# Splitting the four-chunk cache loads of a decode kernel between the queues of SyncE and ScalarE

## The chip, the cores and the metric

The kernel runs on one core of one Trainium2 chip. The metric is the time of one execution on the device, in microseconds (us). Before the change it was 2488.25 us, the median of 3 runs (2488.16 to 2488.78). The engines are written as in the profile: PE (TensorE matmul), PEld (its weight load), DVE (VectorE), ACT (ScalarE), POOL (GpSimd) and SP (SyncE). SPq and ACTq are the instruction queues of SP and ACT where they issue transfers; the transfers themselves run on 16 DMA engines that the core has.

## What is computed

Two rounds of the same two layers on a decode step with batch B = 2, width D = 512: an attention layer over a long cache (32 query heads, 8 heads of K and V, 32768 keys, head width 128), then a small mixer.

```python
x = x + A(layernorm(x))      # A: grouped-query attention over the cache
x = x + M(layernorm(x))      # M: LayerNorm, one token mixed to F = 1792 hidden, gelu, back
x = x + A(layernorm(x))
x = x + M(layernorm(x))

def A(x):
    q = (x @ wq)                                  # 32 heads of 128
    scores = einsum("bhqd,bhkd->bhqk", q, k) * 128 ** -0.5
    o = einsum("bhqk,bhkd->bhqd", softmax(scores), v)
    return o @ wo
```

All values are float32. K and V of one batch and one cache head are 16.8 MB each, and there are 16 such pairs, 537 MB; both rounds read the whole cache (small parts are kept on the chip between the rounds), so that 1061 MB come in over the DMA engines.

## The kernel before

**Units and chunks.** The work on one pair of batch and cache head in one layer is a unit `n`, 0 to 31. Its K and its V are cut into 8 chunks of 4096 keys, 2.1 MB each (`CK`, 16 KB in each of 128 partitions). PE multiplies each K chunk with the unit's queries (`k_chunk`, L481, into `scores`), and each V chunk with the exponentials of the scores (`v_chunk`, L638, into `acc`). On the page, one matmul of the program is two instructions, so a chunk is 16 of them.

**Loads.** All chunks lie in one large tile, `mem`. `load_k` and `load_v` pick cells of it and call `load` (L188), which issues one transfer on SP. In the first part of the program (K of units 0 to 12, V of 0 to 11) and in the last (K of 21 to 31, V of 20 to 30 and the first of 31) a load brings four chunks, 64 KB to a partition; two cell groups (cells 0 to 3, cells 4 to 7) take turns. In the middle part the loads are of one to three chunks and go to more cells. The last V is loaded as four chunks, two chunks, and then five pieces of a half chunk and less (`PIECES`). Weights of two heads at a time are loaded on SP as well (L129, and 32 KB pieces of them at L142).

**Order.** The order of the program is written out by hand. `stream` is the list of loads, sorted by a key; the last loop of the kernel takes one load after the other, issues it, then emits its chunks on PE, and after each chunk `run(t)` emits the other steps that are due at that time: `at(time, step, ...)`. Every engine executes its own instructions in this order. An issue of a transfer therefore stands, on the engine that issues it, behind all that this engine was given before; it also waits by semaphores until PE has read out what lies in the cells.

**One round in the first and last part.** There K of a unit and V of the unit before it alternate. I count positions in chunks from the begin of a unit's K; a round is 16 positions long, for K of unit n+1 and V of unit n:

| position | load issued there | PE reads | ACT is given, after that chunk |
|---|---|---|---|
| 0 to 4 | Ka: K chunks 0 to 3 | them | at 4: exps(n,1), exponentials of the second half of the scores of n |
| 4 to 8 | Va: V chunks 0 to 3 | them | |
| 8 to 12 | Kb: K chunks 4 to 7 | them | |
| 12 to 16 | Vb: V chunks 4 to 7 | them | at 14: exps(n+1,0), those of the first half of n+1 |

A step "at 4" is emitted after the chunk that ends at 4 and ahead of the load that is issued at 4. `exps` is `exponentials` (L518): four activations and four reads of their accumulator on ACT. exps(n+1,0) needs the maximum of all scores of n+1, which two small products on PE give, `max_1` (at 13) and `max_2` (at 14, L510); exps(n,1) needs the transposed scores (`turn_scores`, L516, DVE, at 4), whose tile is free once Vb has been read. Ka and Kb lie in one cell group, Va and Vb in the other. At 0 to 3 there is also the output of the unit before (`out_0` to `out_2`), from 10 on the queries of the next unit (`make_q`). After the last unit of a pair of layer and batch the mixer's gelu tiles (`hidden_tile`, L889, one a position) come on ACT too.

**The end.** The last unit is 31. exps(31,1) are given to ACT when V of unit 30 has been read (`t1 = ahead`), before the load of V chunks 0 to 3 of unit 31 is emitted. After the last V piece come the last output and the last mixer (`last_out`, `last_mixer`).

Of the kernel before, what the change touches and what calls it, by code (L numbers as in the profile page):

```python
# [14 lines left out]
CK = 4096  # L15
# [3 lines left out]
PACK = 4  # L19
# [30 lines left out]
def gqa_mixer_kernel(ctx: ExitStack, tc: tile.TileContext, x, kt, v, wqo, cols, out):  # L50
# [17 lines left out]
    nc = tc.nc  # L68
# [104 lines left out]
    loaded, seen = [0], {0: 0}  # L173
# [12 lines left out]
        return loaded[0] - seen[-(-t // 1)] + (-t) % 1 if t <= now[0] else 0  # L186

    def load(t, src):  # L188
        nc.sync.dma_start(t, src)
        loaded[0] += t.shape[-1] / CK  # L190

    def buffer(m, limit, until):

# [256 lines left out]
    def load_k(n, c, m, limit):  # L450
        layer, b, h = unit_of(n)
        stay = h == keeper and c in KEPT_K
        until = k_done[n, c + m - 1]
        if stay:
            for j in range(m):
                hold(KEPT_K[c + j], 1, k_done[units.index((1, b, h)), c + j])
            bufs = [cells(KEPT_K[c], m)]
        elif limit == RING:
            bufs = spread(m, until, n in (N1 + 1, N2 + 1) and m == 1)
        else:  # L460
            bufs = [buffer(m, limit, until)]
        src, f = piece(kt, b * HKV + h, c, m), 0
        for t in bufs:
            if not (stay and layer):
                load(t, src[:, f : f + t.shape[-1]])
            f += t.shape[-1]
        at = [q for t in bufs for q in quads(t)]
        for j in range(m):
            k_at[n, c + j] = at[j * (JT // QT) : (j + 1) * (JT // QT)]
# [81 lines left out]
    def load_v(n, c, m, limit):  # L551
# [7 lines left out]
        if stay and m > 1:  # L559
            k = KEPT[c][1]  # L560
            own = cells(k, m)
            load(own, src)
            for j in range(m):
                hold(k + j, 1, v_done[units.index((1, b, h)), c + j])
                v_at[n, c + j] = quads(cells(k + j))
            return
        if stay:
            if layer == 0:
                load(own, src[:, :f])
                for j in range(2 if stay > QT else 1):  # L570
                    busy[2 * KEPT[c][1] + j] = v_done[units.index((1, b, h)), c]
            if stay == JT // QT:
                v_at[n, c] = at
                return
            bufs = [half(until)[:, : CK - f]]
        elif limit == RING:
            bufs = spread(m, until, False, PLACE_V.get((n - N1, c)))
        else:
            bufs = [buffer(m, limit, until)]
# [405 lines left out]
    kbeg, k_done, vbeg, v_done, vend_of, v_from, v_to, brings, starts, t = {}, {}, {}, {}, {}, {}, {}, [], [], 0  # L985
# [171 lines left out]
    t = 0  # L1157
# [83 lines left out]
```

## Time and profile before

| what | value |
|---|---|
| median of 3 runs | 2488.25 us |
| span of the profiled execution, first to last instruction | 2486.6 us |
| PE busy | 1413.2 us (57%) |
| DVE busy | 256.6 us (10%) |
| ACT busy | 185.5 us (7%) |
| read from HBM | 1061.19 MB, 427 GB/s over the span |
| chain that ended last, DMA's share | 72% |

The profile is one execution, taken by the hardware profiler; its own time lies 1.65 us under the median of the runs. The page shows the span in 40 slices with the DMA engines' busy share and rate, the queues, the chain of work that ended last, and the costliest groups of instructions. Other views of the same trace list the transfers of a stretch (DMA), the instructions in order of time (timeline), the chain piece by piece, and busy time by stretch (windows). A timeline row reads: start, duration, engine, line, operation, result <- operands, count, and in brackets the idle time before it with what ended it. A row with SPq is the issue of a transfer, not its duration. Sizes in the DMA view are left out for the largest transfers.

### The profile page before, as it was taken

How to read it: one execution, taken by the hardware profiler on the slowest of the kernel's cores; microseconds unless marked ns; L12 is line 12 of the kernel's file. 1: busy time of each engine (PE TensorE's matmuls, PEld its weight loads, DVE VectorE, ACT ScalarE, POOL GpSimd, SP SyncE). 2: the span in 40 equal slices, each digit the busy share in tenths (PEclk: the TensorE clock that was granted, in tenths of full speed). 3: DMA queues.
4: the chain of work that ended last, by engine and by line, in shares of the span. 5: the costliest groups of instructions: out<-in, count | busy, mean ns of one | idle time of the engine just before them, and what ended most of it. 6: DMA issues, size and time to landing. Idle time of an engine off the chain costs nothing.

```text
span 2486.6 us, 20856 instructions
## 1 busy us (share of the span) xinstructions
PE 1413.2 (57%) x9438; PEld 386.1 (16%) x9438; DVE 256.6 (10%) x659; ACT 185.5 (7%) x544; POOL 4.9 (0%) x17
## 2 busy tenths in 40 slices
PE   4544545556555454657677675455555664456546
PEld 1111111111111111112122121111111111111112
DVE  1000000000000000003113110000000000010002
ACT  0000000000000000002012000000000000011002
POOL 0000000000000000000000000000000000000000
PEclk8777777776777777888888887777677777777878
DMA  9999999999999999999999999999999999999996
GB/s 421 434 433 429 433 437 430 434 436 431 427 435 431 436 427 432 431 429 412 431 433 415 429 432 432 434 435 430 436 429 429 429 435 434 428 436 431 434 435 287
DMA packets 30594, 1062.54 MB, mean 427 GB/s; under 512 B 3749, under 2 KB 3753, under 8 KB 4394
## 3 DMA queue, kind: packets, MB, share of 16 engines
q1 hardware_dynamic: 30216, 1061.17, 99.2%
q8 instruction: 74, 1.21, 0.2%
q14 instruction: 14, 0.11, 0.0%
q10 hardware_dynamic: 290, 0.04, 0.0%
HBM read 1061.19 MB, written 0.00 MB: 427 GB/s over the span
## 4 chain that ended last, share of the span: by engine, by line
DMA 72%; PE 26%; DVE 0%; issue 0%; another core or an unknown queue 0%; ACT 0%; SPq 0%; ACTq 0%
DMA mem<-in_v_dram 61%; PE acc L638 20%; DMA mem<-in_kt_dram 10%; PE scores L481 3%; DMA mem<-in_wqo_dram 2%; PE kept L162 1%; PE kept L395 1%; PE small L669 0%; PE small L510 0%; PE bcast L395 0%; PE small L797 0%; PE small L504 0%; PE kept L296 0%; PE kept L849 0%
## 5 line engine op out<-in xcount | busy, mean ns | idle before, releaser
L481 PE MATMUL scores<-mem,small_sb 128*32 128x512 f32 x4096 | 615.7, 724 | 544.5 <-DMA mem<-in_kt_dram 544.4
L638 PE MATMUL acc<-mem,S 128*16 128x512 f32 x4088 | 621.3, 737 | 473.0 <-DMA mem<-in_v_dram 471.3
L481 PEld LDWEIGHTS scores<-mem,small_sb 128*32 128x32 f32 x4096 | 147.2, 127 | 914.6 <-issue 839.2
L521 ACT ACTIVATE S<-S,small_sb 128x128 f32<-128x128 f32 x232 | 119.3, 518 | 1974.6 <-DVE small_sb L512 1377.0
L638 PEld LDWEIGHTS acc<-mem,S 128*16 128x16 f32 x4088 | 132.6, 110 | 839.6 <-issue 699.1
L496 DVE TENSOR_REDUCE small_sb<-scores 128x1 f32<-128x512 f32 x64 | 44.3, 692 | 743.8 <-PE scores L481 743.8
L516 DVE STREAM_TRANSPOSE S<-scores 128x512 f32<-128x512 f32 x64 | 45.5, 710 | 141.4 <-PE acc L638 137.2
L395 PE MATMUL kept<-mem,small_sb 128*2 128x512 f32 x96 | 54.5, 691 | 3.9 <-DMA mem<-in_wqo_dram 2.1
L296 PE MATMUL kept<-mem,small_sb 128*1 128x512 f32 (+1 forms) x236 | 42.1, 597 | 2.7 <-ACT mem L892 2.4
L521 ACT ACTIVATION_READ_ACCUMULATOR S<-S,small_sb 128x1 f32 x232 | 43.3, 187 | 0.0
L506 DVE TENSOR_REDUCE small_sb<-small 1x4 f32<-1x128 f32 x32 | 8.9, 279 | 294.1 <-PE small L504 294.1
L671 DVE RECIPROCAL small_sb<-small 128x4 f32<-128x4 f32 x32 | 5.9, 185 | 321.6 <-PE small L669 321.6
L680 DVE TENSOR_TENSOR small_sb<-small,small_sb 128x4 f32<-128x4 f32 x31 | 5.1, 164 | 299.1 <-PE small L678 299.1
L608 DVE SCALAR_TENSOR_TENSOR S<-acc,small_sb,S 128x128 f32<-128x128 f32 x93 | 32.6, 351 | 3.3
L892 ACT ACTIVATE S<-bcast,small_sb 128x512 f32<-128x512 f32 x28 | 21.6, 778 | 89.9 <-DVE small_sb L761 87.8
L606 DVE TENSOR_SCALAR S<-acc,small_sb 128x128 f32<-128x128 f32 x31 | 10.8, 350 | 146.7 <-PE acc L638 146.7
L162 PE MATMUL kept<-mem,small_sb 48*2 48x512 f32 x32 | 25.2, 929 | 0.0
L421 PE MATMUL small<-small_sb,mem 2*128 2x2 f32 x112 | 14.7, 248 | 17.9 <-DVE mem L417 17.9
L395 PE MATMUL bcast<-mem,small_sb 128*1 128x512 f32 (+1 forms) x40 | 20.9, 640 | 0.0
L678 PEld LDWEIGHTS small<-small_sb,S 128*128 128x128 f32 x62 | 13.2, 266 | 48.7 <-issue 41.9
L797 PE MATMUL small<-small_sb 128*128 128x128 f32 x120 | 18.7, 290 | 0.0
L504 PE MATMUL small<-small_sb 128*1 128x128 f32 x64 | 16.7, 354 | 3.3 <-DVE small_sb L502 3.3
(154 smaller groups left out, 340.9 us busy)
## 6 DMA issues: line engine op xcount, KB each, us to landing
mem<-in_kt_dram SPq DMA_DIRECT2D x14, 4096.0 KB
mem<-in_v_dram SPq DMA_DIRECT2D x11, 4096.0 KB
mem<-in_v_dram SPq DMA_DIRECT2D x13, 2048.0 KB
mem<-in_kt_dram SPq DMA_DIRECT2D x12, 2048.0 KB
mem<-in_kt_dram SPq DMA_DIRECT2D x24, 1024.0 KB
mem<-in_v_dram SPq DMA_DIRECT2D x21, 1024.0 KB
mem<-in_wqo_dram SPq DMA_DIRECT2D x4, 3840.0 KB
mem<-in_wqo_dram SPq DMA_DIRECT2D x3, 4096.0 KB
```

What stands on the lines that cost most here:

```text
L162: nc.tensor.matmul(q_ps[n][:B, :], low[:, j * B : (j + 1) * B], lowered[h][:, j * D : (j + 1) * D], start=(j == 0), stop=False,)
L296: nc.tensor.matmul((rows if to is None else to)[32 * g : 32 * g + b + 1, :], weights if b else weights[:, 1:], row, start=to is not None, ...
L395: nc.tensor.matmul(q_ps[n][:m, :], xnT[:, d, b : b + m], wq_at(h, d), start=(d == 0 and h not in lowered), stop=(d == last),)
L481: nc.tensor.matmul(sc_ps[n, half][32 * g : 32 * g + 32, :], q, kc[k * NG + g], start=(i == 0 and k == 0), stop=(i == PACK - 1 and k == SUB ...
L496: nc.vector.tensor_reduce(mx[n][:, half : half + 1], sc_ps[n, half], axis=AX.X, op=ALU.max)
L504: nc.tensor.matmul(pm[:1, :P], mxa, ident, start=True, stop=True)
L516: nc.vector.transpose(S[half], sc_ps[n, half])
L521: nc.scalar.activation(s[:, :, h], s[:, :, h], AF.Exp, bias=neg[n][:, h : h + 1], scale=SCALE, accum_out=lsum[n][:, half, h : h + 1],)
L608: nc.vector.scalar_tensor_tensor(t, acc[:, k * DH : (k + 1) * DH], mask[:, k : k + 1], t, op0=ALU.mult, op1=ALU.add)
L638: nc.tensor.matmul(acc[32 * g : 32 * g + R * QT, :], S[half][:, col : col + R * QT], vc[q], start=(c == v_from[n] and q < NG), stop=(c == ...
L797: nc.tensor.matmul(p[:, :P], ident, ident, start=True, stop=True)
L892: nc.scalar.activation(hid[key, f], px[key], AF.Gelu_apprx_tanh, bias=shift[key][:, f : f + 1], scale=slope[key][:, f : f + 1],)
```

## The change

`load` splits a load of four chunks into two halves by columns: the first two chunks are issued on SP as before, the other two on ACT. The destination cells, the source and all other loads are the same.

```diff
     def load(t, src):
-        nc.sync.dma_start(t, src)
-        loaded[0] += t.shape[-1] / CK
+        w = t.shape[-1]
+        if w == PACK * CK:
+            nc.sync.dma_start(t[:, : w // 2], src[:, : w // 2])
+            nc.scalar.dma_start(t[:, w // 2 :], src[:, w // 2 :])
+        else:
+            nc.sync.dma_start(t, src)
+        loaded[0] += w / CK
```

So each half has a transfer and a completion of its own: rows of 32 KB, 128 of them, 4.2 MB. The issue on ACT stands in ACT's order at the position of the load in the table above. In the texts below Ka1 is the half of Ka on SP and Ka2 the half on ACT, and so on; V01, V23, V45 and V67 are the chunk pairs of the last V.

## The prediction

> **What bounds the kernel now.** I read the page first (span, DMA row, queues), then the DMA view in three stretches, then the timeline of two loads in the middle, then the chain at the end.
>
> ```profile
> span 2486.6 us, 20856 instructions
> ...
> PE 1413.2 (57%) x9438; PEld 386.1 (16%) x9438; DVE 256.6 (10%) x659; ACT 185.5 (7%) x544; POOL 4.9 (0%) x17
> ...
> DMA  9999999999999999999999999999999999999996
> GB/s 421 434 433 429 433 437 430 434 436 431 427 435 431 436 427 432 431 429 412 431 433 415 429 432 432 434 435 430 436 429 429 429 435 434 428 436 431 434 435 287
> ...
> q1 hardware_dynamic: 30216, 1061.17, 99.2%
> ...
> L892 ACT ACTIVATE S<-bcast,small_sb 128x512 f32<-128x512 f32 x28 | 21.6, 778 | 89.9 <-DVE small_sb L761 87.8
> ```
> ```profile
> mem<-in_kt_dram SPq DMA_DIRECT2D x48
> mem<-in_v_dram SPq DMA_DIRECT2D x47
> ```
>
> The DMA row is 9 in every slice but the last, one queue carries 99.2%, and the rate stays near 432 GB/s. The kernel is bound by bytes. The two rows without a size are the loads that the change splits: 48 of K and 47 of V, 128 rows of 64 KB each, 8.39 MB a load, 797 MB of the 1061. The stretch 100 to 1000 us has, apart from weights, nothing but them; the stretch 1440 to 1530 us has nothing but 4 MB loads, in 32 KB rows, which is the very shape of a half; 1140 to 1200 us is mostly 1 MB loads in 8 KB rows:
>
> ```profile
> DMA packets 7033, 389.13 MB, mean 432 GB/s; under 512 B 824, under 2 KB 824, under 8 KB 824
> ```
> ```profile
> DMA packets 1408, 38.77 MB, mean 431 GB/s; under 512 B 160, under 2 KB 160, under 8 KB 160
> ...
> mem<-in_kt_dram SPq DMA_DIRECT2D x6, 4096.0 KB
> mem<-in_v_dram SPq DMA_DIRECT2D x3, 4096.0 KB
> ```
> ```profile
> DMA packets 3242, 24.67 MB, mean 411 GB/s; under 512 B 359, under 2 KB 359, under 8 KB 359
> ...
> mem<-in_v_dram SPq DMA_DIRECT2D x10, 1024.0 KB
> ```
>
> So 432 GB/s with 64 KB rows, 431 with 32 KB rows, 411 only where rows are far shorter. Half a load alone is 4.194 MB / 432 GB/s = 9.7 us, two halves that share the engines 19.4 us.
>
> Why do the engines never run dry? One unit in the middle (Vb, then Ka, Va, Kb of the next; positions as in the section on the kernel):
>
> ```profile
> 1806.14 0.38 PE L510 MATMUL small<-small_sb 1*128 1x4 f32 x2
> 1806.45 3.63 PE L638 MATMUL acc<-mem,S 128*16 128x512 f32 x32
> ...
> 1808.80 0.19 ACT L521 ACTIVATION_READ_ACCUMULATOR S<-S,small_sb 128x1 f32 x1
> 1810.14 0.33 SPq L189 DMA_DIRECT2D mem<-in_v_dram  x1
> ...
> 1819.89 3.64 PE L481 MATMUL scores<-mem,small_sb 128*32 128x512 f32 x16 [9.81 <-DMA mem<-in_kt_dram]
> ...
> 1827.13 3.61 PE L481 MATMUL scores<-mem,small_sb 128*32 128x512 f32 x32
> ...
> 1830.80 0.33 SPq L189 DMA_DIRECT2D mem<-in_kt_dram  x1
> ...
> 1832.24 0.52 ACT L521 ACTIVATE S<-S,small_sb 128x128 f32<-128x128 f32 x1 [23.25 <-DVE S L516]
> ...
> 1834.16 0.19 ACT L521 ACTIVATION_READ_ACCUMULATOR S<-S,small_sb 128x1 f32 x1
> ...
> 1839.57 3.18 PE L638 MATMUL acc<-mem,S 128*16 128x512 f32 x16 [8.84 <-DMA mem<-in_v_dram]
> ...
> 1849.23 0.33 SPq L189 DMA_DIRECT2D mem<-in_v_dram  x1
> ...
> 1859.23 5.32 PE L481 MATMUL scores<-mem,small_sb 128*32 128x512 f32 x32 [10.06 <-DMA mem<-in_kt_dram]
> ...
> 1870.62 0.33 SPq L189 DMA_DIRECT2D mem<-in_kt_dram  x1
> ...
> 1887.41 0.19 ACT L521 ACTIVATION_READ_ACCUMULATOR S<-S,small_sb 128x1 f32 x1
> ```
>
> Each SPq row is a load issued the moment PE has read its buffer out: 1810.14, 1830.80, 1849.23. The load ahead of it lands some 9 us later (PE starts on it at 1819.89, 1839.57, 1859.23). So the queue holds about 9 us of work whenever a new load joins it. SP can do that because it has nothing else to wait for.
>
> **The change part by part.** *What is removed and added.* 95 issues of SP become 95 of SP and 95 of ACT, 0.33 us each by the SPq rows; ACT is busy 7%, and 95 x 0.33 = 31 us spread over the span lies in its idle time. No byte is added. The rows of these loads go from 64 to 32 KB, which the stretches above price at 432 against 431 GB/s: 797 MB take 1845 or 1849 us. I take **+3 us**, and keep 0 to 7 us (7 for what rounding and the stretch's edges hide).
>
> *Two queues at once* are not in this trace. The slices that hold nothing but these loads run from 427 to 437 GB/s: at 437 the 797 MB would take 1824 us, 21 us less, at 427 1866 us, 21 us more. I take neither: the one queue keeps the 16 engines busy for 99.2% of the span, so there is no pause for a second to fill, and the bytes are the same. As to how the engines share, I take turns row by row, since the profile counts a packet for each row: 1408 packets less the 160 tiny ones are 1248 for 38.77 MB, 31 KB each. So two queues that both have work get half the rate each.
>
> [...]
>
> *The order in which ACT issues* is the real edit. SP still runs ahead, and earlier than now, since half a buffer is free after two chunks. ACT issues in program order behind its exponentials. At position 14 stands exps(n,0), before the issue of the next Ka's second half (Ka2); at 4 stands exps(n,1), before the issue of Va2 and of Kb2, behind it. By the rows, exps(n,0) ends 2.8 us after the products of position 14 (1806.14 to 1808.99), and exps(n,1) 3.6 us after Ka is read (1830.74 to 1834.35). A Ka is now issued at 1870.62; its half on ACT would have to wait for exps that end at 1887.60, 17 us later. A Va is now issued at 1810.14; its half would wait until 1834.35, 24 us later. In the other direction nothing is held up: when ACT comes to Ka2, Va2 or Kb2 the buffer has been read, and behind Vb2, which does wait for PE (position 8), only the exps of position 14 are queued. Where the 14 gelu tiles of a mixer (778 ns each) are spread over the positions after 3, each waits for PE at an earlier position than the issue behind it, so I add nothing. On SP nothing is moved past anything; the weight loads find a shorter queue.
>
> Do the engines run dry? Prices: a half from a cold PE 5.3 us (1859.23, 32 instructions), a hot one 3.6 (1827.13), Kb's second half 6.1 with the query products in it (1864.55 to 1870.62). From issue to first byte, and from last byte to PE:
>
> ```profile
> 0.74 0.39 SPq L129 DMA_DIRECT2D mem<-in_wqo_dram  x1
> ```
> ```profile
> 0.00:5.00 5.00, 0.00 (x0) 0.00 (x0) 1.56 (x6) 1.28 (x1) 0.94 (x10) 1.00 0.69 236
> ```
> ```profile
> 1.19 31.17 DMA mem<-in_kt_dram
> ```
>
> 236 GB/s over 5 us is 1.18 MB, 2.7 us at 432: the first byte moved at 2.3 us, 1.55 us after the issue began. The weights and the first K load are 12.58 MB, 29.1 us: done at 31.4, and the wait ended at 32.36. I take 1.55 us for the start and 1.15 for the landing with PE's own 0.14.
>
> Let Ka2 and Va1 (shared) have their last bytes at 0.
> - SP's Kb1, queued long before, runs alone 0 to 9.7. PE reads Ka2 1.2 to 6.5 and Va1 to 10.1. exps(n,1) end 6.5 + 3.6 = 10.1: ACT issues Va2 and Kb2; SP issues Vb1 at 10.1 (Va1 read). First bytes at 11.65: the engines are **dry for 2.0 us**.
> - Va2 and Vb1 share to 31.1. PE reads Va2 to 37.6 (ACT issues Vb2) and Kb1 to 41.2 (SP issues the next Ka1, moving at 42.8). Kb2 runs alone to 40.8, Vb2 alone to 42.8, then shared with Ka1 to 58.2.
> - PE reads Kb2 42.0 to 48.1 and Vb1 to 52.3. exps(n,0) are over at 55.1: Ka2 could move at 56.7, before 58.2.
> - Ka2 starts at 58.2 and ends at 77.6. In that time SP ends Ka1 (62.2) and has 2.0 us of Va1 left, with Kb1 behind it: 11.7 us of cover, where 11.65 are needed. So the second round has no gap.
>
> One round is then 77.6 us, eight halves of 9.7: the bytes still set it, but the cover has gone from 9 us to 0.05, 1.5 and 1.6 us at three places. There are 23 such rounds (12 in the first stretch, 11 in the last). I charge 0.3 us a round, **7 us**; between 0 and 2.0 in each, 46 us.
>
> *The end.* The last V load of four chunks (V01 on SP, V23 on ACT) is followed by V45 and the pieces V67, on SP. The chain now, and ACT's last exps:
>
> ```profile
> 2437.71 3.65 PE acc L638 x32
> ...
> 2442.15 27.95 DMA mem<-in_v_dram
> ...
> 2470.14 0.45 PE kept L654 x8
> ```
> ```profile
> 2446.21 0.19 ACT L521 ACTIVATION_READ_ACCUMULATOR S<-S,small_sb 128x1 f32 x1
> ```
>
> Now the last piece lands and PE needs 0.45 us for it. After the change V23 waits for exps(31,1), which end 5.0 us after the last Vb is read (2441.36 to 2446.40). On the clock above, with V01 in the place of Ka1: Vb2's bytes end at 58.2, PE has read it at 64.7, ACT issues V23 at 69.7, moving at 71.3. SP has meanwhile finished V01 (60.2) and V45 (69.9), and 1.4 us of V67; the rest shares with V23: V67 ends at 87.9, **V23 last, at 89.3**. PE then still has six chunks to read: from 90.4, 5.4 + 3.6 + 3.6, to 103.0, where the present order would end at 89.3 + 1.15 + 0.45 = 90.9. That is **+12 us**. With all of V01 still to come at 58.2, V23 would end 6 us before the pieces and the cost be 6; with 12 us or more, nothing.
>
> *Sum.* 3 + 7 + 12 = +22 us on the profiled span: 2486.6 + 22 = 2508.6. The median shown, 2488.25, lies 1.65 above that span, so **2510 us**. The start costs nothing by the same count: the weights share with K's first second half, but 20 MB are queued by then, and the bytes set the end.
>
> **Rivals.** [...]
> [...]
> *Dry in every round*: the 2.0 us gap of the first round comes back, because the landing or the issue on ACT takes longer than I took (the margins of 1.5 us go too): 46 + 12 + 3, about 2549. For it: the margins are that thin. Against: after a gap SP's queue stands fuller.
> *No change*: V23 gets its bytes early, because SP's queue still holds 12 us or more when ACT comes to it, and no gap comes back: 2488 to 2492. For it: the count of the end stands on one clock for 24 units; against: SP has only V45 and V67 left there.
>
> **How the numbers follow.** Forecast (2500 to 2530) 0.45, in turn 0.12, dry in every round 0.13, no change 0.17, faster 0.13. The no-change case lies within 0.2% (5 us, about what a measurement of this kernel can tell from none), the three others above it: faster 0.13, same 0.17, slower 0.70. The range, 2485 to 2546, leaves out most of the faster case and the far end of the dry one.
>
> **What would show it.** Right: two hardware queues, the second with about 398 MB (95 x 4.19); ACTq issues of Va2 and Kb2 back to back just behind the exps that follow Ka; DMA slices still at 9; at the end PE reading six chunks without a break after an ACT load landed. Wrong: a steady rate of 435 or more (faster), 8s in the DMA row (dry), or a last piece that still lands last (no change). A sharing that is not even would spoil the clock.

## The result, and the profile after

| what | before | after |
|---|---|---|
| median | 2488.52 us (4 runs) | 2545.20 us (4 runs, 2543.5 to 2547.68) |
| ratio to before | | 1.0228, 95% interval 1.0213 to 1.0242 |
| span of the profiled execution | 2486.6 us | 2544.5 us |

The change costs 56.7 us, 2.3%. It was forecast as slower, at 2510 us: the direction is right, but of the 56.7 us the forecast had only 22. The measured 2545.2 lies at the upper edge of the range (2485 to 2546). The page after, with the rows that answer to those shown of before:

```profile
span 2544.5 us, 21026 instructions
...
DMA  9999999999999999999999999999999999999995
GB/s 419 430 426 431 429 419 426 410 432 432 413 408 410 429 430 389 431 431 421 430 428 414 431 432 426 404 419 432 428 423 430 420 428 429 410 407 429 405 428 234
...
q1 hardware_dynamic: 30216, 662.72, 60.9%
q10 hardware_dynamic: 13970, 398.50, 36.7%
```

The change does what it says: a second hardware queue carries 398.5 MB, 95 halves of 4.19 MB. The two queues together still show 9 in nearly every slice, and a tenth hides what matters: the rate, which stood at 427 to 437 GB/s in the slices of the rounds, now falls to 419, 410, 408, 389 in some. In the DMA view of the stretch 100 to 1000 us the mean is 420 GB/s where it was 432; 432 - 420 is 2.8%, 25 us in these 900.

```profile
DMA packets 13133, 378.36 MB, mean 420 GB/s; under 512 B 1512, under 2 KB 1512, under 8 KB 1512
q1 hardware_dynamic: 6910, 197.53, 51.2%
q10 hardware_dynamic: 6193, 180.39, 47.0%
```

One round of the timeline after (start, duration, engine, ...). PE starts on Ka2 at 656.00, on Va2 at 682.03, on Kb2 at 696.95:

```profile
644.52 0.33 SPq L191 DMA_DIRECT2D mem<-in_kt_dram  x1
...
656.00 5.10 PE L486 MATMUL scores<-mem,small_sb 128*32 128x512 f32 x32 [10.68 <-DMA mem<-in_kt_dram]
...
662.88 0.34 ACTq L192 DMA_DIRECT2D mem<-in_v_dram  x1
663.33 0.37 ACTq L192 DMA_DIRECT2D mem<-in_kt_dram  x1
664.60 0.33 SPq L191 DMA_DIRECT2D mem<-in_v_dram  x1
...
682.03 5.72 PE L643 MATMUL acc<-mem,S 128*16 128x512 f32 x32 [16.63 <-DMA mem<-in_v_dram]
...
687.83 0.34 ACTq L192 DMA_DIRECT2D mem<-in_v_dram  x1
691.26 0.33 SPq L191 DMA_DIRECT2D mem<-in_kt_dram  x1
...
696.95 5.10 PE L486 MATMUL scores<-mem,small_sb 128*32 128x512 f32 x32 [5.77 <-DMA mem<-in_kt_dram]
...
705.78 0.33 SPq L191 DMA_DIRECT2D mem<-in_v_dram  x1
...
706.69 0.33 ACTq L192 DMA_DIRECT2D mem<-in_kt_dram  x1
```

The order is as told before the run: two ACTq issues back to back, Va2 and Kb2, behind the exponentials that follow Ka, at 662.88 and 663.33. And in front of them the engines run dry. The windows view (stretch, length, busy time of PE, PEld, DVE, ACT and POOL, the clock, then DMA share and GB/s as the last two figures) of the same place:

```profile
656.00:660.00 4.00, 4.00 (x24) 1.03 (x28) 0.00 (x0) 0.00 (x0) 0.00 (x0) 0.63 1.01 434
660.00:664.00 4.00, 4.00 (x44) 0.98 (x36) 1.31 (x2) 1.40 (x5) 0.00 (x0) 1.00 0.51 188
664.00:668.00 4.00, 0.91 (x10) 0.30 (x2) 0.35 (x2) 0.77 (x4) 0.00 (x0) 1.00 0.86 344
```

From 660 to 664 us the engines moved 188 GB/s, from 664 to 668 344: (431 - 188) x 4 / 431 + (431 - 344) x 4 / 431 = 3.1 us are missing, of which some come back in the next window (508 GB/s from 668 to 672 us, at a DMA share of 1.18: a row is counted whole where it starts). In the same view cut into stretches of 6 us, 6 from 100 to 1000 us and 7 from 1620 to 2440 us lie below 330 GB/s (116 to 328, so 1.4 to 4.4 us missing in each), and every one of the 13 stands where Va2 is issued. That is about every second round. Together these places miss some 31 us.

The end, as the chain of waits shows it (start, duration, what):

```profile
2489.14 5.10 PE acc L643 x32
...
2497.43 17.99 DMA mem<-in_v_dram
...
2515.46 11.54 PE acc L643 x88
```

The half of the last V on ACT (V23) is issued at 2497.43, 3.2 us after the last Vb has been read (2489.14 + 5.10 = 2494.24), is the last that PE waits for, and PE then reads six chunks in one go: five and a half in the 11.5 us of the last row, the rest by 2527.8 us. Before the change it needed 0.45 us after the last landing. V23 isn't the very last to land: in the DMA view, 0.8 MB of the small pieces on SP's queue move after 2514.5 us, and nothing of V23 does. But PE takes the chunks in order, so they cost it no further wait.

### The profile page after: what moved, and what is told of

Same layout as the page of the kernel before. It is cut to its first block, busy times and chain, and to the rows that moved or that the text cites. A ratio compares the mean times of both kernels' runs of the same rounds, so it can differ in the third digit from the quotient of the medians.

```text
span 2544.5 us, 21026 instructions
## 1 busy us (share of the span) xinstructions
PE 1388.8 (55%) x9438; PEld 371.6 (15%) x9438; DVE 256.2 (10%) x659; ACT 184.7 (7%) x544; POOL 4.9 (0%) x17
## 4 chain that ended last, share of the span: by engine, by line
DMA 74%; PE 21%; DVE 3%; ACT 1%; issue 1%; ACTq 0%; SPq 0%; POOL 0%
DMA mem<-in_kt_dram 63%; PE scores L486 12%; DMA mem<-in_v_dram 11%; PE acc L643 7%; DVE small_sb L501 1%; PE kept L400 1%; ACT S L526 1%; DVE S L521 0%; PE small L426 0%; PE small L515 0%; PE bcast L400 0%; DVE mem L422 0%; PE small L704 0%; ACT mem L876 0%; DVE small_sb L517 0%
## 5 line engine op out<-in xcount | busy, mean ns | idle before, releaser
L643 PE MATMUL acc<-mem,S 128*16 128x512 f32 x4088 | 610.7, 726 | 645.8 <-DMA mem<-in_v_dram 643.9
L486 PEld LDWEIGHTS scores<-mem,small_sb 128*32 128x32 f32 x4096 | 140.2, 128 | 841.0 <-DMA mem<-in_kt_dram 462.4
L914 DVE SCALAR_TENSOR_TENSOR acc<-S,small_sb,acc 128x512 f32<-128x512 f32 x24 | 18.1, 755 | 2.5
L426 PEld LDWEIGHTS small<-small_sb,mem 2*128 2x128 f32 x112 | 13.5, 186 | 30.6 <-DVE mem L422 27.3
L802 PEld LDWEIGHTS small<-small_sb 128*128 128x128 f32 x120 | 15.2, 190 | 13.7 <-issue 13.6
L674 PE MATMUL small<-small_sb 128*128 128x4 f32 x64 | 12.4, 265 | 8.7 <-DVE small_sb L673 8.7
L400 PEld LDWEIGHTS kept<-mem,small_sb 128*2 128x2 f32 x96 | 9.5, 100 | 48.1 <-issue 45.4
```

Source lines behind the costliest of these rows:

```text
L400: nc.tensor.matmul(q_ps[n][:m, :], xnT[:, d, b : b + m], wq_at(h, d), start=(d == 0 and h not in lowered), stop=(d == last),)
L426: nc.tensor.matmul(pt[:, r * m : (r + 1) * m], q_row[n][:m, r * DH : (r + 1) * DH], ident[:m, :m], start=True, stop=True,)
L486: nc.tensor.matmul(sc_ps[n, half][32 * g : 32 * g + 32, :], q, kc[k * NG + g], start=(i == 0 and k == 0), stop=(i == PACK - 1 and k == SUB ...
L643: nc.tensor.matmul(acc[32 * g : 32 * g + R * QT, :], S[half][:, col : col + R * QT], vc[q], start=(c == v_from[n] and q < NG), stop=(c == ...
L802: nc.tensor.matmul(p[:, :P], ident, ident, start=True, stop=True)
L914: nc.vector.scalar_tensor_tensor(h if f == FT - 1 else acc, h, w, acc, op0=ALU.mult, op1=ALU.add)
```

## The experiments

Three theories stood at the outset. A: the cost is the place of the issues in ACT's order (dry engines in the rounds, a half that lands last at the end). B: it is the halved rows. C: it is the sharing of the engines by two queues. Later A was put more narrowly, as A2: only the late issue of Va2 counts. Its rivals were R1, by which both late issues (Ka2 too) take their share, and R3, by which a late issue has a fixed price whatever the sizes.

**Both halves on SP** takes ACT out and leaves the split.

```diff
-            nc.scalar.dma_start(t[:, w // 2 :], src[:, w // 2 :])
+            nc.sync.dma_start(t[:, w // 2 :], src[:, w // 2 :])
```

> Both halves of every four-chunk load are issued on SP; ACT issues none. Theory A (the cost is the place of the issues in ACT's order: the engines run dry in each round, and one half lands last at the end): as before, 2487 to 2493 us, rate 431 to 433 GB/s from 100 to 1000 us. Theory B (twice as many rows of half the length cost it): some 17 us above before, 2505, at a rate near 428. Theory C (two queues that share the engines move fewer bytes a second): as A, 2487 to 2493.

Measured: 2495.55 us, ratio to before 1.0029 (1.0017 to 1.0040). Of the 56.7 us the split itself costs 7.2, more than A allowed (up to 2493) and far less than B asked for (2505); B is out as the main cause. The rate moved from 432 to 431, and there is no dip:

```profile
DMA packets 13449, 387.91 MB, mean 431 GB/s; under 512 B 1536, under 2 KB 1536, under 8 KB 1536
```

**Exponentials behind the issues.** In the rounds, exps(n,0) are emitted half a chunk after the issue of Ka2 and exps(n,1) half a chunk after that of Va2.

```diff
+            ordinary = 0 < n < N1 - 1 or N3 + 2 <= n < NU - 1
 ...
-                at(e, exponentials, n, 0)
+                at(e + (2.5 if ordinary else 0), exponentials, n, 0)
 ...
-            at(t1, exponentials, n, 1)
+            at(t1 + (0.5 if ordinary else 0), exponentials, n, 1)
```

> SP and ACT issue as in the change, but in the rounds the exponentials stand behind the issue of Ka2 and of Va2 in ACT's order instead of ahead of them. A: the dips in each round go, what remains is the end, about 9 us: 2496 to 2503 us, 430 GB/s or more from 100 to 1000 us. B: 9 + 17, 2514. C: the rate stays near 420 to 428, 2510 to 2540.

Measured: 2509.75 us, 1.0083 (1.0068 to 1.0098): 35.5 us of the loss are gone, with both queues still at work. The time lies above A's range (2496 to 2503), which had left out the 7 us of the split and taken 9 us for the end, and it is about the lowest that C allowed (2510). The rate decides: from 100 to 1000 us the two queues together move as many bytes as SP does alone with the same rows, so C is out too:

```profile
DMA packets 13448, 387.80 MB, mean 431 GB/s; under 512 B 1539, under 2 KB 1539, under 8 KB 1539
```

**The last V load whole, on SP.** The load of four chunks of unit 31 isn't split; the rest is as in the change.

```diff
-    def load(t, src):
+    def load(t, src, whole=False):
-        if w == PACK * CK:
+        if w == PACK * CK and not whole:
 ...
-                load(t[:, :k], src[:, f : f + k])
+                load(t[:, :k], src[:, f : f + k], n == NU - 1)
```

> As the change, but the one four-chunk load of the last V is whole and on SP. A, with the half on ACT as what lands last: 8 to 10 us less than the change, 2535 to 2537. If the end costs nothing, 2543 to 2547, as the change.

Measured: 2532.08 us, 1.0182 (1.0165 to 1.0199), 13.1 us less than the change, some 3 to 5 more than expected. The end has its old form again:

```profile
2478.05 35.84 DMA mem<-in_v_dram
...
2513.92 0.45 PE kept L659 x8
```

**Both of these edits together.**

> Both edits together: exponentials behind the issues of Ka2 and Va2, and the last V load whole on SP. A: all of the loss is gone but a few us, 2488 to 2494. B: 2505. C: 2500 to 2530.

Measured: 2499.26 us, 1.0044 (1.0027 to 1.0061). 45.9 of the 56.7 us are gone. My 2494 was missed by 5 us. Of what is left, 7.2 us are the split itself, as on SP alone; the 3.7 us between that run (2495.55) and this one weren't followed up, though one dip of 2.2 us is left in its stretch 1620 to 2440 us.

**One of the two moves alone**, to see which late issue costs what. First exps(n,1) only (the `t1` line above):

> As the change, but only exps(n,1) stand behind the issue of Va2 (exps(n,0) stay ahead of Ka2). Theory A2 (the engines run dry once a round, between the end of Kb1, which SP runs alone, and the issue of Va2, so that only this place counts): as with both moved, 2506 to 2513 us. Rival R1 (both late issues take their share): about half of the 35 us comes back, 2522 to 2535.

Measured: 2521.23 us, 1.0131 (1.0114 to 1.0148): 24.0 us come back. Then exps(n,0) only (the `e` line):

> As the change, but only exps(n,0) stand behind the issue of Ka2 (exps(n,1) stay ahead of Va2). A2: nothing comes back, 2540 to 2549 us. R1: 2522 to 2535.

Measured: 2534.64 us, 1.0184 (1.0169 to 1.0200): 10.6 us come back. A2 was too narrow. Each move lies outside A2's range for it (R1's, 2522 to 2535, misses the first by a microsecond and holds the second); 24.0 + 10.6 = 34.6 us is within a microsecond of the 35.5 that both gave. Two thirds of the loss in the rounds come back with the one move, one third with the other. That isn't a count of where the engines stand: in the change itself all 13 low stretches lie at Va2, so most of what an earlier Ka2 gives back must have been lost there, a few steps later. The place before Ka2 can go dry too. A dip of the kernel with only exps(n,1) moved shows it: Ka2 is issued (784.86) just behind the first activation of exps(n,0), and the rate falls in front of it (windows view, last figure):

```profile
784.47 0.52 ACT L526 ACTIVATE S<-S,small_sb 128x128 f32<-128x128 f32 x1 [44.78 <-DVE small_sb L517]
784.86 0.33 ACTq L192 DMA_DIRECT2D mem<-in_kt_dram  x1
```
```profile
780.00:784.00 4.00, 4.00 (x37) 1.39 (x37) 0.57 (x4) 0.00 (x0) 0.00 (x0) 1.00 0.76 324
784.00:788.00 4.00, 1.26 (x14) 0.45 (x17) 0.16 (x1) 2.11 (x8) 0.00 (x0) 1.00 0.84 295
788.00:792.00 4.00, 4.00 (x40) 0.99 (x32) 1.29 (x4) 0.00 (x0) 0.00 (x0) 1.00 1.14 492
```

**Other shares: three chunks on SP, one on ACT**, and the reverse. The order on ACT is that of the change.

```diff
-            nc.sync.dma_start(t[:, : w // 2], src[:, : w // 2])
-            nc.scalar.dma_start(t[:, w // 2 :], src[:, w // 2 :])
+            nc.sync.dma_start(t[:, : 3 * CK], src[:, : 3 * CK])
+            nc.scalar.dma_start(t[:, 3 * CK :], src[:, 3 * CK :])
```

> As the change, but SP brings three chunks of four and ACT one, with ACT's order as in the change. A2: what SP runs alone while ACT waits grows from 9.7 to 14.6 us, more than the 10.7 us between the last packets of Ka2 and the first of Va2, so the dips go: 2498 to 2512 us with the rows and the end. Rival R3 (each late issue on ACT costs its own, whatever the sizes): as the change, 2540 to 2549.

Measured: 2505.15 us, 1.0067 (1.0052 to 1.0082), as A2 has it: no dip is left, 430 GB/s from 100 to 1000 us, although every issue on ACT stands where it stood in ACT's order. The edit helps twice: SP has more to move meanwhile, and PE has only one chunk to read before exps(n,1), so that in a round of this kernel the issue of Va2 comes 5.4 us after PE's start on the part of Ka on ACT (567.19 to 572.61), where the change has 6.9 (656.00 to 662.88). So here, with three chunks on SP to move in the meantime, the late issues cost nothing that shows in the rate; R3 is out. With 1 in the place of 3:

> As the change, but SP brings one chunk of four and ACT three. A2: SP's cover falls to 4.9 us, so the engines are dry for some 4.9 us more in each of 23 rounds: 2545 + 110 = 2655 us, 2615 to 2700. R3: as the change, 2540 to 2549.

Measured: 2827.7 us, 1.1362 (1.1339 to 1.1385). The sign is right, the size isn't: 282 us instead of 110. Two dry places of one round of this kernel, ahead of Va2 and, in the second fence, ahead of Ka2 (windows view; the last two figures are DMA share and GB/s):

```profile
916.00:920.00 4.00, 0.00 (x0) 0.00 (x0) 0.00 (x0) 0.00 (x0) 0.00 (x0) 0.50 0.89 385
920.00:924.00 4.00, 2.45 (x12) 0.59 (x16) 0.00 (x0) 0.00 (x0) 0.00 (x0) 0.50 0.36 152
924.00:928.00 4.00, 4.00 (x28) 0.93 (x24) 0.00 (x0) 0.00 (x0) 0.00 (x0) 0.63 0.01 4
928.00:932.00 4.00, 4.00 (x40) 0.91 (x32) 1.31 (x2) 0.06 (x1) 0.00 (x0) 1.00 0.00 0
932.00:936.00 4.00, 0.15 (x4) 0.00 (x0) 0.16 (x1) 2.05 (x8) 0.00 (x0) 1.00 0.76 258
```
```profile
896.00:900.00 4.00, 4.00 (x22) 0.93 (x18) 0.13 (x1) 0.00 (x0) 0.00 (x0) 0.54 0.44 184
900.00:904.00 4.00, 4.00 (x40) 1.09 (x36) 0.54 (x3) 2.20 (x8) 0.00 (x0) 1.00 0.78 270
```
```profile
900.46 0.33 ACTq L192 DMA_DIRECT2D mem<-in_kt_dram  x1
...
921.55 3.64 PE L486 MATMUL scores<-mem,small_sb 128*32 128x512 f32 x16 [16.13 <-DMA mem<-in_kt_dram]
...
932.16 0.35 ACTq L192 DMA_DIRECT2D mem<-in_v_dram  x1
```

Ahead of Va2 the engines are dry for some 11 us (by the DMA shares, 916 to 936 us). I had taken only the smaller cover; but the part on ACT is now three chunks, so PE reads longer before exps(n,1): from PE's start on it to the issue it is 932.16 - 921.55 = 10.6 us, where the change has 662.88 - 656.00 = 6.9. Cover 4.9 us less and wait 3.7 us more are 8.6 us a round beyond the change, about 200 in 23 rounds. The other 80 us weren't followed up, but the round above shows where to look: ahead of Ka2 (issued at 900.46) another (431 - 184) x 4 / 431 + (431 - 270) x 4 / 431 = 3.8 us are missing. If every round lost that, which wasn't added up, it would be 87 us (an estimate).

**What is it in the split that costs 7 us on SP alone?** Four loads of one chunk, all on SP, in the place of the two halves:

```diff
+            for k in range(PACK):
+                nc.sync.dma_start(t[:, k * CK : (k + 1) * CK], src[:, k * CK : (k + 1) * CK])
```

> Every four-chunk load is cut into four loads of one chunk (16 KB rows), all on SP. If each added row or transfer costs the same as in the split in two on SP (7.2 us for one cut): 3 x 7.2 = 21.6 us above before, 2506 to 2514 us. If the 7 us of the split in two came from elsewhere (the end, the start): 2494 to 2499.

Measured: 2510.04 us, 1.0088 (1.0071 to 1.0104), 21.7 us, three times the price of one cut. This doesn't part rows from transfers. A cut by partitions, again in the place of the two halves, keeps the rows at 64 KB:

```diff
+            nc.sync.dma_start(t[: P // 2], src[: P // 2])
+            nc.sync.dma_start(t[P // 2 :], src[P // 2 :])
```

> Every four-chunk load is cut in two by partitions (0 to 63, 64 to 127), rows of 64 KB as before the change, both on SP. If the price of the split is that of the rows: as before, 2487 to 2490 us. If it is that of the transfer (95 more issues and completions): 2494 to 2497.

Measured: 4560.91 us, 1.8328 (1.8301 to 1.8355). That answers another question: with each half going to 64 neighbouring partitions the rate was half, 207 GB/s from 1000 to 1100 us against 432 from 100 to 1000 us before. With `t[::2]` and `t[1::2]` instead:

> Every four-chunk load is cut in two by partitions, even and odd ones, so that each half still spans the whole memory; rows of 64 KB as before the change, both halves on SP. If the price of the split on SP (7.2 us) is that of its shorter rows: 2487 to 2490 us. If it is that of the transfer (95 more issues and completions): 2494 to 2497. If a half of the partitions is slow wherever it lies: far above, as the cut at partition 64.

Measured: 2493.83 us, 1.0022 (1.0012 to 1.0031). By its time alone, 5.5 us above before, it would be the transfers. The trace says otherwise. The DMA view of 100 to 1000 us for the even and odd halves (twice the transfers, rows of 64 KB) and for the quarters (16 KB):

```profile
DMA packets 7748, 388.82 MB, mean 432 GB/s; under 512 B 1543, under 2 KB 1543, under 8 KB 1543
```
```profile
DMA packets 26123, 384.95 MB, mean 428 GB/s; under 512 B 2949, under 2 KB 2949, under 8 KB 2949
```

With 64 KB rows the rate is nearly that of before, 388.82 MB in the stretch against 389.13; with 32 KB it is 387.91, with 16 KB 384.95. The stretch 1620 to 2440 us says the same more clearly: 354.60 MB before, 354.61 with even and odd halves, 353.34 with the two halves on SP. Most of the 5.5 us of the even and odd halves is lost once, at the start, where SP issues the first K load only at 14.94 us (1.19 before) and the engines stand for about 4 us; why it is issued so late wasn't followed up:

```profile
14.94 0.58 SPq L191 DMA_DIRECT2D mem<-in_kt_dram  x1
```
```profile
12.00:16.00 4.00, 1.16 (x4) 1.00 (x4) 1.20 (x7) 0.00 (x0) 0.00 (x0) 1.00 0.04 7
```

So in the steady rounds the price goes with the rows: (389.13 - 387.91) / 389.13 is 0.31%, 5.8 us on the 1845 us of these loads (6.6 us by the other stretch).

## Why the prediction was right and wrong

**The bound** of the kernel before was right: bytes on 16 engines that hardly pause (99.2%). So was the reading that ACT's order is the edit that counts, and that Va2 and Kb2 would go out together behind exps(n,1) and Ka2 behind exps(n,0).

**The rows** were taken at +3 us, with 0 to 7 kept. Measured 7.2 on SP alone, some 6 of them by the rate. The term was low; the measured cost lies just past its upper bound.

**Two queues at once** were taken as neither gain nor loss. That holds: 387.80 MB from two queues against 387.91 from one, in the same 900 us. *Faster*, given 0.13, needed 435 GB/s or more; no run shows that two queues raise the rate: both moved 431.

**The end** was worked out as +12 us, and 13.1 us came back without it (10.5 on top of the moved exponentials). The mechanism was right, six chunks that PE has to read after waiting for V23, but that the sizes agree so well is in part luck: the clock had V23 issued 5.0 us after the last Vb, and it was 3.2, because ACT issued it 0.28 us after the start of the first activation of exps(31,1) (2497.15 to 2497.43), while the last of them began only at 2498.68; and the clock had V23 land behind the last pieces, while it landed ahead of the smallest ones.

**The rounds** are the step that failed. I charged 0.3 us in each of 23 rounds, 7 us; the moved exponentials give back 35.5 us, 1.5 us a round. The dry gap of 2.0 us in the first line of the clock was of the right size (1.4 to 4.4 us are missing at the 13 places), and three lines later it was argued away: "the second round has no gap", because SP would have 2.0 us of Va1 left over and Kb1 behind it, 11.7 us of cover. Those 2.0 us came from the second line, where Vb2 runs alone before Ka1 joins it.

The trace shows no such lead. Counted from the issue of Va2 (662.88), Ka1 is issued after 28.4 us (691.26; the clock had 31.1), and PE begins Kb2 after 34.1 us (696.95; the clock had 31.9). So Kb2 is done only about when Ka1 is ready to move, and Vb2 gets hardly any time alone. That Ka1 comes earlier goes back one line further up. I let Va2 and Vb1 start together, at 11.65; in the trace ACT issues Va2 1.7 us ahead of Vb1 (664.60), since it doesn't wait for its exponentials to end (662.88, while the last of them began at 664.17). And Vb1, which joins busy engines, has no row under way before 668 us (DMA view, stretches 666 to 668 and 668 to 670 us):

```profile
q10 hardware_dynamic: 17, 0.56, 64.4%
```
```profile
q1 hardware_dynamic: 16, 0.52, 60.6%
q10 hardware_dynamic: 15, 0.49, 56.9%
```

Va2 is done first, PE reads it and Kb1 that much sooner, and the rest of Vb1 shares with Kb2. Why PE begins Kb2 2.2 us later than in the clock stays open. Queue by queue (DMA view, stretches 687 to 694 and 654 to 660 us):

```profile
DMA packets 124, 3.10 MB, mean 442 GB/s; under 512 B 29, under 2 KB 29, under 8 KB 29
q10 hardware_dynamic: 109, 3.08, 102.4%
```
```profile
DMA packets 83, 2.56 MB, mean 426 GB/s; under 512 B 5, under 2 KB 5, under 8 KB 5
q1 hardware_dynamic: 78, 2.56, 98.8%
```

ACT's queue has the engines to itself in the first stretch, and in the second, behind Ka2, SP has only Kb1. The cover is one half, 9.7 us, as in the first round, and the wait is longer: the gap returns. Why it returns in only about every second round wasn't worked out. That was the rival *dry in every round*, given 0.13 and 2549 us, 46 + 12 + 3; measured were 35 + 13 + 7. Its reason wasn't quite the one I gave: not a longer landing or issue, but a lead that didn't build up. Margins of 0.05 and 1.5 us in a clock that was off by 2 to 3 us at two of its steps were no ground to hold its chance at an eighth. With one move alone 24 us came back at the place with the margin of 0.05 (Va2) and 11 at that with 1.5 (Ka2). The sign that was named for this rival, 8s in the DMA row, could not show it: 1.5 us in a round of some 80 us is 2%, and the row counts in tenths.

**How two queues share.** The kernel with one chunk on SP (16 KB rows) and three on ACT (48 KB) tells turns row by row from turns by whole parts of a load. Stretch 936 to 944 us, both at work (a row is counted whole where it starts, hence 114% in the two shares and the 494 GB/s):

```profile
DMA packets 113, 3.95 MB, mean 494 GB/s; under 512 B 0, under 2 KB 0, under 8 KB 0
q10 hardware_dynamic: 64, 3.15, 90.8%
q1 hardware_dynamic: 49, 0.80, 23.4%
```

64 rows of ACT and 49 of SP went through side by side, in bytes 3.15 to 0.80 MB. In the DMA view by 2 us, 16 rows of ACT and 15 or 16 of SP stand in each stretch from 938 to 944 us. Whole parts in turn would show one queue alone for some 4.9 us (2.1 MB of SP at 431 GB/s) or 14.6 us (6.3 MB of ACT), an estimate. The sharing is nearly row by row here, as I took it. *In turn*, given 0.12, was to have a half served whole before the other queue's turn; no run shows that. Of these two queues the one with the 48 KB rows got most of the bytes.

## What to carry to other kernels

A load that is issued on an engine with other work is issued in that engine's order (here Va2 at 662.88, just behind the start of exps(n,1) at 662.60): look for what stands ahead of it there, and what that waits for, before counting anything else. What the lateness cost here went with how much the other queue still had to move (2505 us with three chunks of four on SP, 2545 with two, 2828 with one), so write that cover down next to the wait, at each place, and where they are within a microsecond or two, give the dry case as much weight as the covered one. And look at the last load on its own: in the rounds late issues could cost nothing (no dip with three chunks on SP), at the end the one late half that PE waited for last cost 13.1 us.

## What the runs showed of the hardware

- Two queues shared the 16 engines nearly row by row, not byte by byte: with one chunk on SP and three on ACT, 64 rows of 48 KB on ACT's queue and 49 of 16 KB on SP's in 936 to 944 us, 3.15 to 0.80 MB.
- Transfers to partitions 0 to 63 and to 64 to 127 in turn moved 207 GB/s with the engines counted as fully busy; to the even and the odd partitions in the same way, 432 (100 to 1000 us). The stretch 1000 to 1100 us of the former (last two figures: DMA share, GB/s):

```profile
1000.00:1100.00 100.00, 28.57 (x182) 7.68 (x186) 2.22 (x7) 1.16 (x5) 0.00 (x0) 0.58 1.00 207
```

  So it was half the rate for blocks of 64 neighbouring partitions (207 GB/s) and the full rate for 64 that are spread (432). What makes the difference wasn't shown.
- The rate fell a little as the rows got shorter, all on SP's queue: 389.13 MB in 900 us at 64 KB, 387.91 at 32 KB, 384.95 at 16 KB.
- In the change ACT issued a transfer that stands behind activations soon after the first of them had started, not when they were over. Exps(n,1), four activations, began at 662.60 and the last of them at 664.17; Va2, behind them in ACT's order, was issued at 662.88.
- In one round of the change the transfer that joined busy engines got its first rows later than the one that found them dry: Va2, issued at 662.88, had 7 rows under way before 664 us (DMA view), Vb1, issued at 664.60, none before 668.
